# Attention and SwiGLU on one core: turning q and k of the last three sequences on VectorE instead of TensorE

## The chip, the cores and the metric

The kernel runs on one core of a Trainium2 chip. The metric is the device time of one execution in microseconds (us), as the median over several runs. The engines are named as the profile names them: PE is TensorE, with its weight loads (PEld) counted apart; DVE is VectorE, ACT is ScalarE, POOL is GpSimd, SP is SyncE, which here only issues DMAs (its queue is SPq). SBUF and PSUM have 128 partitions; matmuls write to PSUM, and DVE and ACT empty it.

## What is computed

Eight sequences of 448 rows with 12 heads of 64 columns. Queries and keys are normed row by row, attention follows, and the result of all heads, side by side, is the input of a SwiGLU layer:

```python
q_n = q / sqrt(mean(q*q) + 1e-6) * g_q        # k_n likewise, with g_k
attn = softmax(q_n @ k_n.T / sqrt(64))
x = (attn @ v), heads side by side            # 3584 rows of 768
xn = x / sqrt(mean(x*x) + 1e-6) * rms_g
out = (silu(xn @ w_gate) * (xn @ w_val)) @ w_out     # 768 -> 1536 -> 768
```

All data are float32.

## The kernel before, in words

**Groups and blocks.** Two heads make a group `g`, six groups a sequence `b` (`divmod(g, NPAIR)`), 48 groups in all. The main loop (line 1805) goes over the groups, one block of work each. From the second sequence on, a block begins with the attention of its group (`step`, line 677, seven parts: the scores of 64 keys against all 448 queries for both heads, the weighted sum of the group before, the exponentials), and the rest of the block is filled with pieces of the feed-forward layer of the sequence before (`fill`, line 1645). In block `g` the scores of group `g` are taken, the weighted sums of group `g - 1`, and groups `g + 1` to `g + 3` are made ready.

**Order by hand.** Every engine executes in the order in which the program issues. `pe(fn)` issues one piece of PE work and moves a clock `now["t"]` by one; `after(n, fn)` puts other work off by `n` such steps, so that it is issued behind later pieces. A block in the middle of a sequence has three calls of `fill`, about a third of its feed-forward work each.

**q and k before.** `load_pair` (line 407) loads rows 0 to 383 of q and k of a group, three rows to a partition; the last 64 rows of all heads of a sequence, the rests, are loaded once a sequence (`load_rests`, line 435). A q load has runs of 768 bytes (one DMA per group), a k load runs of 256 bytes (two DMAs). `squares` (line 484) squares on ACT, sums per row on DVE, and takes the power -1/2 on POOL (`rms_qk`, line 510); `norm_q` (line 517) scales q on POOL, `norm_k` (line 524) scales k on ACT, six instructions; `norm_rests` (line 450) does the same for the rests. `turn` (line 532) then turns rows into columns on PE: three transposes against the identity for q and one for the rests of both, and three for k, seven a group, into a PSUM bank, from which ACT copies them to `qT` (line 550, with the gains `gqk` as a column of scales) and `kT` (lines 551 and 553). The two turns of a group are two pieces of PE work in the block before its scores.

**Attention.** `scores` (line 655) multiplies 64 columns of kT by qT, two matmuls in the two halves of the array; `exps` (line 662) takes the exponential, without a maximum, since a bound on the scores was checked; `weighted` (line 666) multiplies by v. The sums of the exponentials are added up on POOL (`later_sums`, line 705) and over partitions on PE (`totals`, line 684).

**Feed-forward.** Gate and value products are made by a scheme with fewer multiplications (`product`, line 1180, line 1191 its matmuls, eight to a product), with additions on DVE and copies on ACT that empty the three PSUM banks for it (`ps_f`). The output layer has three forms; of these, the one in quadrants (`out_quads`, line 1476, matmuls in line 1532, `finish` with additions on POOL) runs under the attention of sequences 5 and 7 too. The weights, ready made, stream in from a scratch area in DRAM (`ask`, line 1042, DMAs in line 1070): a piece is asked for when a place in a ring of 22 pieces is free. All these DMAs are issued on SP, in one order with the loads of q, k and v and the stores of the output.

**v and the output.** v lies as q does, three rows to a partition, and the output rows (`store`, line 1347) follow that order.

## Time and profile before

| | |
|---|---|
| timed runs | 1516.35, 1512.67, 1513.35 us; median 1513.35 us |
| profiled execution, first to last instruction | 1514.0 us (no time around this span is given) |
| share of the span: PE, PEld, DVE, ACT, POOL | 98%, 76%, 69%, 40%, 49% |
| granted PE clock, mean | 0.997 |
| DMA share of 16 engines, by the SP queue | 69.4% |
| bytes moved, mean rate | 322.51 MB, 213 GB/s |

The profile is one execution. Busy times of an engine are the sums of its instructions' durations; matmuls overlap one another, so that a PE that is always busy is not yet a PE at its peak, and what a matmul costs is better read from the distance between starts in the timeline. A row of instruction groups reads: line, engine, operation, output and inputs with shapes, count, then the busy time in us and the mean ns of one, then the engine's idle time just before them and what ended it. A row of a stretch of time reads: from and to, length, busy us and count of PE, PEld, DVE, ACT and POOL, the granted clock, the DMA share, GB/s. A row of waits reads: who waited for whom, us in total, how often, the longest. A row of DMA issues reads: destination and source, queue, count, KB each, median us from issue to landing.

### The profile page before, as it was taken

What the parts mean: (1) busy time and instruction counts of PE and PEld (TensorE: products, weight loads), DVE (VectorE), ACT (ScalarE), POOL (GpSimd) and SP (SyncE); (2) the same over time, 40 slices, a digit from 0 to 9 for tenths busy, and PEclk for the clock granted to TensorE, in tenths of its full rate; (3) what the DMA queues carried; (4) which work ended last, traced back from release to release, by engine and by line L of the source; (5) the groups of instructions that cost most, each with busy time, mean ns of one, the idle gap of its engine ahead of it and who ended that gap; (6) DMA issues with size and microseconds to landing.
All of it is one profiled execution on the core that took longest, in us unless ns stands there. A gap on an engine that the chain in (4) does not pass through costs nothing.

```text
span 1514.0 us, 25709 instructions
## 1 busy us (share of the span) xinstructions
PE 1478.8 (98%) x8732; PEld 1154.0 (76%) x8732; DVE 1037.7 (69%) x1826; ACT 602.2 (40%) x1377; POOL 741.3 (49%) x708
## 2 busy tenths in 40 slices
PE   8999999999899999999999999999999999999997
PEld 4344445678755888878888888768888789899997
DVE  5788999699944697874568555535668655684664
ACT  6856764344323433234343443443542433101100
POOL 6867997556423454564535643445645731021002
PEclk9999999999999999999999999999999999999999
DMA  7758675776667899996558855585558655587675
GB/s 200 227 159 252 174 247 174 228 249 206 224 219 224 266 316 312 301 291 180 163 150 257 244 176 153 165 255 159 153 153 255 216 162 139 165 292 234 174 228 180
DMA packets 302176, 322.51 MB, mean 213 GB/s; under 512 B 81620, under 2 KB 243668, under 8 KB 302036
## 3 DMA queue, kind: packets, MB, share of 16 engines
q1 hardware_dynamic: 301108, 320.58, 69.4%
q8 instruction: 72, 1.18, 0.3%
q14 instruction: 68, 0.56, 0.1%
q10 hardware_dynamic: 800, 0.20, 0.1%
q0 software_dynamic: 128, 0.00, 0.0%
HBM read 266.90 MB, written 53.77 MB: 212 GB/s over the span
## 4 chain that ended last, share of the span: by engine, by line
PE 84%; DVE 8%; DMA 3%; issue 1%; SPq 1%; POOL 1%; ACT 0%; DVEq 0%; POOLq 0%
PE ff L1191 37%; PE ff L1532 13%; PE sc L659 7%; PE av L674 7%; PE ff L1604 6%; PE ff L1461 5%; PE tr L545 2%; PE den L692 1%; PE den L607 1%; PE sc L563 1%; PE av L590 1%; PE ff L1334 1%; DVE l L1406 1%; DMA w<-kept 1%; DVE w L1091 1%
## 5 line engine op out<-in xcount | busy, mean ns | idle before, releaser
L1191 PE MATMUL ff<-x,w 128*128 128x224 f32 x1296 | 259.6, 353 | 1.4 <-DVE pb L1212 1.1
L714 POOL TENSOR_TENSOR es<-es,e 128x448 f32<-128x448 f32 x205 | 253.4, 1236 | 13.6
L1191 PEld LDWEIGHTS ff<-x,w 128*128 128x128 f32 x1296 | 242.7, 190 | 5.4 <-DVE pb L1212 1.4
L659 PE MATMUL sc<-qT,kT 64*64 64x448 f32 x1176 | 231.0, 539 | 0.7 <-DVE x L744 0.7
L674 PE MATMUL av<-e,vt 64*64 64x448 f32 x984 | 193.1, 538 | 0.0
L664 ACT ACTIVATE e<-sc 128x448 f32<-128x448 f32 x294 | 154.2, 547 | 72.6 <-PE sc L659 57.1
L1191 PE MATMUL ff<-xs,w 128*128 128x224 f32 x832 | 165.0, 353 | 2.9 <-issue 1.6
L1191 PEld LDWEIGHTS ff<-xs,w 128*128 128x128 f32 x832 | 155.7, 190 | 6.2 <-issue 3.0
L644 POOL TENSOR_TENSOR ss<-ss,rd 128x448 f32<-128x448 f32 x40 | 47.1, 1178 | 207.2 <-ACT rd L643 206.5
L709 POOL TENSOR_TENSOR es<-e 128x448 f32<-128x448 f32 x41 | 49.2, 1200 | 192.3 <-ACT e L664 192.3
L659 PEld LDWEIGHTS sc<-qT,kT 64*64 64x64 f32 x1176 | 79.2, 133 | 82.1 <-issue 60.1
L1532 PE MATMUL ff<-w,l 128*128 128x192 f32 x630 | 117.8, 328 | 3.7 <-DVE pa L1567 1.7
L515 POOL TENSOR_TENSOR rs<-ms,mhalf 128x12 f32<-128x12 f32 (+1 forms) x50 | 115.9, 2319 | 4.2
L1212 DVE TENSOR_TENSOR pc<-ff,l 128x448 f32<-128x448 f32 x56 | 34.8, 622 | 115.7 <-PE ff L1191 80.9
L1604 PE MATMUL ff<-x,w 128*128 128x448 f32 x288 | 111.8, 541 | 0.0
L1532 PEld LDWEIGHTS ff<-w,l 128*128 128x128 f32 x630 | 103.8, 190 | 8.7 <-DVE pa L1567 2.9
L674 PEld LDWEIGHTS av<-e,vt 64*64 64x64 f32 x984 | 66.0, 133 | 41.6 <-issue 41.6
L1604 PEld LDWEIGHTS ff<-x,w 128*128 128x128 f32 x288 | 53.3, 190 | 51.1 <-issue 48.2
L1191 PE MATMUL ff<-top_x,w 128*128 128x224 f32 x440 | 91.1, 356 | 0.0
L1209 DVE TENSOR_TENSOR pb<-ff,pb 128x448 f32<-128x448 f32 x84 | 52.3, 623 | 56.1 <-PE ff L1191 50.3
L1191 PEld LDWEIGHTS ff<-top_x,w 128*128 128x128 f32 x440 | 81.8, 190 | 11.3 <-issue 8.5
L1191 PE MATMUL ff<-l,w 128*128 128x224 f32 x416 | 83.6, 353 | 1.1 <-DVE pc L1212 1.1
(212 smaller groups left out, 2806.1 us busy)
## 6 DMA issues: line engine op xcount, KB each, us to landing
w<-kept SPq DMA_DIRECT2D x380, 256.0 KB, 3.5
w<-kept_q SPq DMA_DIRECT2D x350, 192.0 KB, 3.8
w<-kept_o SPq DMA_DIRECT2D x150, 192.0 KB, 3.6
kept_q<-w SPq DMA_DIRECT2D x63, 192.0 KB, 3.9
qk<-in_q_dram SPq DMA_DIRECT2D x48, 192.0 KB, 3.7
qk<-in_k_dram SPq DMA_DIRECT2D x96, 96.0 KB, 3.7
raw<-in_moe_w_gate_dram SPq DMA_DIRECT2D x24, 384.0 KB, 4.8
raw<-in_moe_w_val_dram SPq DMA_DIRECT2D x24, 384.0 KB, 4.4
```

The source lines that it names most:

```text
L515: nc.gpsimd.tensor_tensor(st["rs", g][:, cols], ms, mhalf[:, cols], ALU.pow)
L644: after(m, lambda: (nc.gpsimd.tensor_tensor(ss, ss, rd, ALU.add), st.update({("summed", b): hp})))
L659: nc.tensor.matmul(ps[r, 0:S], lhsT=st["kT", g][r, keys_of(i)], rhs=st["qT", g][r, :], start=True, stop=True)
L664: nc.scalar.activation(e, ps[:, 0:S], ACT.Exp)
L674: nc.tensor.matmul(st["av", g][own(j), 0:S], lhsT=vt, rhs=st["e", g, i][r], start=i == 0, stop=i == PARTS - 1, skip_group_check=True)
L709: nc.gpsimd.tensor_tensor(st["es", g], st["e", g, 0], st["e", g, 1], ALU.add)
L714: nc.gpsimd.tensor_tensor(st["es", g], st["es", g], st["e", g, i], ALU.add)
L1191: nc.tensor.matmul(bank[:, w * HT:(w + 1) * HT], lhsT=data(key)[:, (2 * w + c) * 128:(2 * w + c + 1) * 128], rhs=a[left][:, c, :], start=o ...
L1209: nc.vector.tensor_tensor(T[name], ps[:, 0:S], T[name], ALU.add)
L1461: nc.tensor.matmul(ps, lhsT=left_o(b, which, LEFT_O[name], c), rhs=data(("wo", b, name, c)), start=first and c == 0, stop=c == NFP - 1, sk ...
L1532: nc.tensor.matmul(ps, lhsT=a[:, j, :], rhs=data(key)[:, n % 2 * HW:(n % 2 + 1) * HW], start=start and j == 0, stop=j == KG - 1, skip_grou ...
L1604: nc.tensor.matmul(bank[w][:, 0:S], lhsT=data(key)[:, c * 128:(c + 1) * 128], rhs=st["x", 0][:, 3 * half + c, :], start=half == c == 0, st ...
```

## The change

For the last three sequences (`b >= 5`, groups 30 to 47, `TURNED = 5`):

- A head's 448 rows are loaded 14 to a partition on 32 partitions, and by halves of 32 columns: partition block (head, half), 32 partitions each. q and k of a group become eight DMAs of 448 runs of 128 bytes, issued one per step of PE work, from four steps after the block's start.
- Each block of 32 partitions by 32 columns is then turned where it lies by one VectorE block transpose over 448 columns, one for q (in place) and one for k (into `kT`). q's columns come out in the order (row within partition, partition), and one ACT instruction reorders them, reading in steps of 32 words, and applies the gains. k's order is kept, and v is loaded in the same order of keys.
- The sum of squares is by halves. ACT exchanges the halves' sums between partitions (eight small copies), POOL adds them, takes the power over 21 columns and scales q over 448 columns. k isn't scaled: its factor goes into the exponential as a column of scales.
- No rests are loaded or normed for these sequences; v comes in four DMAs of 32 partitions; output rows are stored in the sequence's own order.
- q, k, v and the rests of all sequences now lie in one tile, `yard`, at places worked out by hand; for the first five sequences with as many buffers as before.
- The two turns are no longer pieces of PE work, so a block has two steps fewer. `squares` of group `g + 2` is issued behind the q turn of group `g + 1`, and v is loaded one block later (for group `g + 1` in block `g`).

The diff, cut to its core:

```diff
+    TURNED = 5
+    NB = S // 32
+    yard = slots.tile([128, AT_OTHER + PER_B], F32, name="yard")
...
+    def load_turned(g):
+        b, hp = divmod(g, NPAIR)
+        qk = st["qk", g] = spot(g % 3 * 2 * S, 2 * S).rearrange("p (a n) -> p a n", a=2)
+        def load(i, h, e):
+            to = (1 - h) * D + 32 * e
+            nc.sync.dma_start(out=blocks(qk[to:to + 32, i]),
+                              in_=(q, k)[i][b, 2 * hp + h].rearrange("(p c) d -> p c d", c=NB)[:, :, 32 * e:32 * e + 32])
+        for n in range(8):
+            after(4 + n, lambda n=n: load(n // 4, n // 2 % 2, n % 2))
...
+    def squares_turned(g):
...
+        for i in range(2):
+            sq = new_sq()
+            nc.scalar.activation(sq, qk[:, i], ACT.Square)
+            after(1, lambda i=i, sq=sq: nc.vector.tensor_reduce(out=ms[:, 0, i * NB:(i + 1) * NB], in_=blocks(sq), axis=AX_X, op=ALU.add))
...
+        def other():
+            for at in (0, 64):
+                nc.scalar.copy(ms[at:at + 32, 1, both], ms[at + 32:at + 64, 0, both])
+                for to, of in ((every, every), (first, second)):
+                    nc.scalar.copy(ms[at + 32:at + 64, 1, to], ms[at:at + 32, 0, of])
+                nc.scalar.copy(ms[at + 32:at + 64, 0, first], ms[at + 32:at + 64, 0, second])
+        def total():
+            nc.gpsimd.tensor_tensor(ms[:, 0, both], ms[:, 0, both], ms[:, 1, both], ALU.add)
+            nc.gpsimd.tensor_scalar(ms[:, 0, both], ms[:, 0, both], D * 1e-6, None, ALU.add)
+        def root():
+            nc.gpsimd.tensor_tensor(rs, ms[:, 0, both], mhalf, ALU.pow)
+            nc.gpsimd.tensor_tensor(blocks(qk[:, 0]), blocks(qk[:, 0]), rs[:, 0:NB].unsqueeze(2).to_broadcast([128, NB, 32]), ALU.mult)
+        after(2, other)
+        after(3, total)
+        after(3, root)
+    def turn_q(g):
...
+        q = st["qk", g][:, 0]
+        nc.vector.transpose(out=blocks(q), in_=blocks(q))
+        after(1, lambda: nc.scalar.activation(st["qT", g].rearrange("p (i n) -> p i n", n=NB), q.rearrange("p (n i) -> p i n", i=32),
+                                              ACT.Copy, scale=gqk[:, 0:1]))
+    def turn_k(g):
...
+        nc.vector.transpose(out=st["kT", g].rearrange("p (n s i) -> p s n i", s=2, i=32),
+                            in_=st["qk", g][:, 1].rearrange("p (s n i) -> p s n i", s=2, i=32))
...
     def exps(g, i, ps):
         e = st["e", g, i] = e_pool.tile([128, S], F32, name="e")
-        nc.scalar.activation(e, ps[:, 0:S], ACT.Exp)
+        if turned(g):
+            nc.scalar.activation(e, ps[:, 0:S], ACT.Exp, scale=st["rs", g][:, NB + i:NB + i + 1])
+        else:
+            nc.scalar.activation(e, ps[:, 0:S], ACT.Exp)
...
+    def turn_for(g, i):
+        if turned(g):
+            (turn_q, turn_k)[i](g)
+        else:
+            pe(lambda: turn(g, i))
...
         if hp:
             fill()
             norm_k(g + 1, 0)
-            squares(g + 2, 0)
-            squares(g + 2, 1)
-            pe(lambda: turn(g + 1, 0))
+            if not turned(g + 2):
+                squares(g + 2, 0)
+                squares(g + 2, 1)
+            turn_for(g + 1, 0)
+            if turned(g + 2):
+                squares(g + 2, 0)
             norm_k(g + 1, 1)
             some_rests(g)
             fill()
-            pe(lambda: turn(g + 1, 1))
+            turn_for(g + 1, 1)
             fill(hold=g % 2 == 1)
```

More of the change, by code (lines that the diff above doesn't have):

```diff
@@ new lines, in load_v_turned @@
+    def load_v_turned(g):
+        b, hp = divmod(g, NPAIR)
+        vt = st["v", g] = spot((AT_QK + 2 * PAIR, AT_V1)[g % 2], S).rearrange("p (n d) -> p n d", d=D)
+        for h in range(2):
+            rows = v[b, 2 * hp + h].rearrange("(p s n) d -> s p n d", s=2, n=NB // 2)
+            for half in range(2):
+                to = across(h).start + 32 * half
+                nc.sync.dma_start(out=vt[to:to + 32], in_=rows[half])
+    def squares_turned(g):
+        qk, n = st["qk", g], 2 * NB
+        ms = st["ms", g] = spot(AT_RS, 2 * n).rearrange("p (a n) -> p a n", a=2)
+        rs = st["rs", g] = spot(AT_RS + (4 + g % 2) * NB + g % 2 * NB // 2, NB + NB // 2)
+        for i in range(2):
+            sq = new_sq()
+            nc.scalar.activation(sq, qk[:, i], ACT.Square)
+            after(1, lambda i=i, sq=sq: nc.vector.tensor_reduce(out=ms[:, 0, i * NB:(i + 1) * NB], in_=blocks(sq), axis=AX_X, op=ALU.add))
+        every, first, second = slice(0, NB), slice(NB, NB + NB // 2), slice(NB + NB // 2, n)
+        both = slice(0, NB + NB // 2)
+        def other():
[13 more added lines that the diff above has]
+        after(3, root)
@@ L450, in norm_rests @@
     def norm_rests(b, lo, hi):
-        if b >= B:
+        if b >= TURNED:
             return
@@ L487, in squares @@
             return
+        if turned(g):
+            if i == 0:
+                squares_turned(g)
+            return
         n = 2 * NK
@@ L524, in norm_k @@
     def norm_k(g, half):
-        if g >= NG:
+        if g >= NG or turned(g):
             return
@@ L1878, in safe_scores @@
         st["block"] = now["t"]
-        after(2, lambda g=g: load_v(g + 2))
+        for n in (1, 2):
+            if turned(g + n) == (n == 1):
+                after(2, lambda g=g + n: load_v(g))
         if hp:
@@ L1894, in safe_scores @@
         fill(2)
-        pe(lambda: turn(g + 1, 0))
+        turn_for(g + 1, 0)
         norm_k(g + 1, 1)
@@ L1900, in safe_scores @@
         squares(g + 2, 1)
-        pe(lambda: turn(g + 1, 1))
+        turn_for(g + 1, 1)
         fill(len(todo))
```

70 lines of the change are left out of this document (52 added, 18 removed).

## The prediction

> **What bounds the kernel now.** I read the page's busy times first, then the table of busy time by stretches, then what TensorE (PE) waited for, then its timeline. The page says that PE is the fullest engine, which alone proves little, because its busy time is modelled:
>
> ```profile
> PE 1478.8 (98%) x8732; PEld 1154.0 (76%) x8732; DVE 1037.7 (69%) x1826; ACT 602.2 (40%) x1377; POOL 741.3 (49%) x708
> ```
>
> The change touches the groups (head pairs) 30 to 47. I asked for the stretch in which their transposes lie, whole, then for the two transposing lines in it, and for two shorter stretches:
>
> ```profile
> 745.00:1260.00 515.00, 512.77 (x3278) 431.12 (x3277) 318.21 (x548) 205.26 (x482) 254.60 (x239) 1.00 0.64 192
> 745.00:1260.00 515.00, 17.79 (x108) 14.05 (x108) 1.00 0.64 192
> 745.00:1260.00 515.00, 4.91 (x18) 2.54 (x18) 1.00 0.64 192
> 1020.00:1110.00 90.00, 90.00 (x569) 77.89 (x568) 53.31 (x85) 40.58 (x97) 48.43 (x49) 1.00 0.55 162
> 1110.00:1200.00 90.00, 89.33 (x613) 76.43 (x612) 71.65 (x129) 31.64 (x78) 51.96 (x45) 1.00 0.67 210
> ```
>
> The columns are PE, weight loads, DVE, ACT, POOL, granted clock, DMA share and GB/s. PE is idle for 515.0 - 512.77 = 2.2 us here, at full clock. The longest of its waits is this one:
>
> ```profile
> PE ff L1532 <- DVE pa L1567: 1.0, 2, 0.5
> ```
>
> So nothing but PE sets the pace of these 515 us, and PE work taken out of them shortens the kernel as long as no other engine or queue comes late. The second and third rows are the transposes of lines 545 and 549: 108 + 18 = 126 of them, seven for each of 18 groups, so the stretch holds exactly the transposes that go.
>
> **What is removed from PE.** Their busy time, 17.79 + 4.91 = 22.7 us, is not what they cost, since matmuls overlap. The timeline gives the cost as the distance between starts:
>
> ```profile
> 1043.31 1.68 PE L1191 MATMUL ff<-xs,w 128*128 128x224 f32 x8
> 1044.82 0.49 PE L545 MATMUL tr<-ident,qn 128*128 128x128 f32 x3
> 1045.15 0.27 PE L549 MATMUL tr<-ident,rest 128*128 128x128 f32 x1
> 1045.26 4.71 PE L1191 MATMUL ff<-xs,w 128*128 128x224 f32 x24
> ...
> 1051.32 0.49 PE L545 MATMUL tr<-ident,qk 128*128 128x128 f32 x3
> 1051.64 1.68 PE L1191 MATMUL ff<-top_x,w 128*128 128x224 f32 x8
> ```
>
> The q turn takes 1045.26 - 1044.82 = 0.44 us, the k turn 1051.64 - 1051.32 = 0.32 us, together 0.76 us a group and 18 x 0.76 = 13.7 us. Scores, weighted sums and denominators keep their matmuls, seven parts a group with the same shapes, so 13.7 us is all that PE can give. An eight-matmul product takes 1044.82 - 1043.31 = 1.51 us, which I need below as the measure of how late an engine that empties PSUM may be: there are three banks for the products.
>
> **What ScalarE (ACT) gets and loses.**
>
> ```profile
> L664 ACT ACTIVATE e<-sc 128x448 f32<-128x448 f32 x294 | 154.2, 547 | 72.6 <-PE sc L659 57.1 <-PE av L674 6.8 <-PE den L607 2.4
> L530 ACT ACTIVATE qk<-qk,rs 128x64 f32<-128x64 f32 x246 | 67.5, 344 | 0.0
> L912 ACT ACTIVATE raw<-raw 128x384 int32<-128x384 uint32 x72 | 40.7, 565 | 0.0
> L493 ACT ACTIVATE sq<-qk 128x384 f32<-128x384 f32 x96 | 45.0, 517 | 1.6 <-DMA qk<-in_k_dram 1.5
> L550 ACT ACTIVATE qT<-tr,gqk 128x448 f32<-128x448 f32 x48 | 30.3, 632 | 106.5 <-PE tr L549 106.5
> L567 ACT ACTIVATE e<-sc,rs 128x448 f32<-128x448 f32 x42 | 23.3, 638 | 13.3 <-PE sc L563 13.3
> L551 ACT COPY kT<-tr 128x64 f32<-128x64 f32 x40 | 8.1, 202 | 0.0
> ```
>
> Gone per group: six scalings of k (6 x 0.344), qT (0.632), the small copy of kT (0.202) and two squares (2 x 0.517), 3.9 us. I give no credit for the large copy of kT and the rests' work, which go too. New: two squares over 448 columns (0.517 x 448/384 = 0.60 each), eight small copies (at most 0.202 each, 1.6), seven exponentials that now take a scale from a column (0.638 against 0.547: 7 x 0.09 = 0.64), and the reordering of q. That last one reads in steps of 128 bytes, which no ACT row shows. Its lower end is L550's 0.632, the same size and the same column of scales; L912, which reads every second word, takes 565 ns against L493's 517, so a step costs little there. Its upper end comes from VectorE, the only engine here that reads in such steps:
>
> ```profile
> L597 DVE STREAM_TRANSPOSE rd<-rd 128x448 f32<-128x448 f32 x41 | 26.2, 639 | 55.1 <-ACT rd L699 54.8
> L598 DVE RECIPROCAL few<-rd 128x14 f32<-128x14 f32 x48 | 11.6, 243 | 1.6
> L496 DVE TENSOR_REDUCE ms<-sq 128x6 f32<-128x384 f32 x96 | 48.4, 543 | 29.3 <-ACT sq L493 29.3
> ```
>
> L598's 243 ns for 14 elements, were all of it the step, would make 448 x 17.4 ns = 7.8 us. I take 0.7 us, near L550, since 243 ns is about what any tiny instruction costs. ACT then has 1.2 + 1.6 + 0.64 + 0.7 = 4.1 us for the 3.9 and more that it loses, at 40.58 of 90 us busy: no change. The Trainium skill (SBUF — State Buffer, in "Door 1: The DMA port swizzle") speaks against this choice: SBUF works in 16-byte lines, and each access that crosses to a new line pays a penalty, of a size that it does not give. L912's step stays inside its lines, so no ACT row here tests the rule. By it the reordering lies nearer its upper end, and that is the slower rival below.
>
> The exponentials keep pace: by L664's row ACT sits idle 72.6/294 = 0.25 us before each, nearly always for PE's scores, and each grows by 0.09.
>
> **VectorE (DVE).** Two block transposes at L597's 0.639 = 1.28 us more per group; the two reductions grow by 448/384, 2 x 0.09 = 0.18 us. Together 1.5 us in a block of about 29 us (515 us / 18). Ahead of the transposes in DVE's order stand additions that empty PSUM; behind them stand others, and the next block's scores wait for kT and qT. In the gate and value stages DVE is busy 53.31 of 90 us, and k is turned about a third of a block, some 8 us of PE work, before its first use: that cover makes it free. In the output stage that works by quadrants (line 1532) DVE is at 71.65 of 90 and PE already waits for it (1.0 us above). Two such stages fall in this stretch; the chain of waits shows their first pieces, and the last matmul of the second one's weights comes from PE's timeline:
>
> ```profile
> 791.32 7.82 PE ff L1532 x48
> 1134.39 7.82 PE ff L1532 x48
> ```
>
> ```profile
> 1197.57 1.14 PE L1532 MATMUL ff<-w,l 128*128 128x192 f32 x6
> ```
>
> That is 64 us a stage, about four blocks in all. There the 1.5 us may cost nothing (they fit in DVE's gaps) or all of themselves, 4 x 1.5 = 6 us. I take 1.5 us in all, nearer to nothing, because the wait that exists is 1.0 us over the whole stretch.
>
> **GpSimd (POOL).**
>
> ```profile
> L714 POOL TENSOR_TENSOR es<-es,e 128x448 f32<-128x448 f32 x205 | 253.4, 1236 | 13.6
> L515 POOL TENSOR_TENSOR rs<-ms,mhalf 128x12 f32<-128x12 f32 x46 | 110.5, 2403 | 3.8
> ```
>
> The power goes from 12 to 21 columns, between 2.4 and 2.4 x 21/12 = 4.2 us; the scaling of q becomes one instruction over 448 columns, at most L714's 1.236, for two over 192; one tiny addition is new. That is under +3.0 us a group, even with nothing deducted for the two, on an engine at 254.60 of 515 us. It now waits for ACT's eight copies, which wait for DVE's reductions, and the additions of the output stage queue behind; but q is next touched a whole block later. Cost nothing.
>
> **The queue of DMA issues (SP).** Three q/k loads and two v loads become eight and four. Here is one block of the quadrant stage, where this queue is fullest, with the next block's first weights:
>
> ```profile
> 1146.97 1.31 SPq L432 DMA_DIRECT2D vt<-in_v_dram  x2
> 1148.33 8.59 SPq L1070 DMA_DIRECT2D w<-kept_q  x16
> 1158.19 2.12 SPq L1358 DMA_DIRECT2D out_dram<-y  x3
> 1160.40 9.42 SPq L1070 DMA_DIRECT2D w<-kept_q  x19
> 1170.09 0.38 SPq L414 DMA_DIRECT2D qk<-in_q_dram  x1
> 1170.57 1.27 SPq L418 DMA_DIRECT2D qk<-in_k_dram  x2
> 1171.94 1.50 SPq L1070 DMA_DIRECT2D w<-kept_q  x3
> 1177.55 1.32 SPq L432 DMA_DIRECT2D vt<-in_v_dram  x2
> 1178.92 4.15 SPq L1070 DMA_DIRECT2D w<-kept_q  x8
> ```
>
> From 1146.97 to the next v load at 1177.55 the queue issues for 24.6 of 30.6 us. New loads at 1.27/2 = 0.64 us each, v at 0.66: 8 x 0.64 + 4 x 0.66 - (0.38 + 1.27 + 1.31) = 4.8 us more, which still fits into the 6.0 us free. Weights are issued up to 1183 us and used up to 1198 us, so this queue runs about 14 us ahead, and being a few us late costs nothing. The moved bytes hardly matter:
>
> ```profile
> qk<-in_q_dram SPq DMA_DIRECT2D x48, 192.0 KB, 3.7
> qk<-in_k_dram SPq DMA_DIRECT2D x96, 96.0 KB, 3.7
> ```
>
> k's 256-byte runs land in the same 3.7 us as q's 768-byte runs, and a group's q and k are under 0.5 MB of the some 5 MB that a block moves. They are loaded two blocks ahead.
>
> **Sum.** 1514.0 - 13.7 + 1.5 = 1501.8 us on the profiled execution's span. The profile gives no time around that span; the three timed runs have their median 0.65 us below it, at 1513.35. Forecast: 1501.2 us.
>
> **Rivals.**
> *The issue queue becomes the bound.* If a load of 448 runs of 128 bytes on 32 partitions holds SP twice as long as a k load, 1.3 us, a quadrant block gets 8 x 1.3 + 2.6 - 3.0 = 10.0 us more for 6.0 free, and blocks are 0.8 us shorter: 4.8 us late per block, 9.6 us by the end of each of the two stages. The lead of 14 us at a stage's end, less 3.7 us of landing, would just cover that; if it is half as long inside the stage, 7 us, it covers 3.3, and PE gives back 2 x 6.3 = 12.6 us: 1513.8 us. For it: the queue is 80% full there. Against: issue time has grown slowly, 0.38 us for 256 runs and 0.64 for 384. The Trainium skill (DMA: Bandwidth & Descriptors, Specifications) asks for at least 512 bytes per transfer for line rate; by that the new loads are slow too, but k's 256-byte runs, already under it, show no later landing. 8%.
>
> *Slower: ACT's reordering holds PSUM.* ACT works in order, and the copies that empty the products' banks queue behind it. With three banks of 1.51 us, ACT may be late by two products, 3.0 us. Beyond that each us stops PE in each of 18 groups. It eats the 13.7 us at 3.8 us per reordering, and is slower by over 0.3% from 4.0 us on; at 5 us the time is 1501.2 + 18 x 2 = 1537 us. For it: the 7.8 us bound. Against: L912. 8%.
>
> *Nothing gained.* The transposes fill time in which PE would wait anyway, for instance for weights: 1513 us. The 2.2 us of idle time speak against it; for it, weights could arrive only just in time, which such a row doesn't show. 4%.
>
> *Every transpose costs its full busy time*, 22.7 us and not 13.7: 1492 us. The starts 0.11 us apart speak against it. 2%.
>
> **How the numbers follow.** The forecast has 78%; its own range is from 1499 (DVE costs nothing, and half a us of scatter) to 1506 (DVE costs all its 6 us). The range of 8 in 10 keeps both ends and takes in most of the first rival: 1498 to 1511. About 0.3%, 4.5 us, is what a measurement of this kernel can tell from no change, so faster means under 1508.8. Faster: forecast 78% and the last rival 2%, 80%. Same: 8% + 4% = 12%. Slower: 8%.
>
> **What would show it.** Right: no transposing matmul after about 750 us; PE's idle time in the stretch from there to the last scores still at 2 to 5 us; the stretch shorter by some 12 to 14 us. The reordering near 0.7 us, the block transposes near 0.64 us, q/k loads near 0.7 us each on SP. Wrong: PE waiting for ACT in the products (the second rival), for a landing of weights in the quadrant stages (the first), or for qT or kT at the front of a block, which I priced at nothing.

## The result, and the profile after

The changed kernel takes 1502.32 us (median of five runs, 1502.07 to 1507.69) against 1512.67 us for the kernel before in the same comparison (five runs, 1511.27 to 1516.35): a ratio of 0.9926, 95% interval 0.9911 to 0.9941. The forecast was 1501.2 us, with a range from 1498 to 1511. The profiled execution took 1502.07 us, 1.8 us more than its span of 1500.3 us.

The busy times of the page after, then of two stretches (columns as before). The first is the old one, cut to match the shorter kernel; the other is a piece of the quadrant stage:

```profile
PE 1466.1 (98%) x8606; PEld 1141.5 (76%) x8606; DVE 1056.0 (70%) x1856; ACT 609.7 (41%) x1371; POOL 758.6 (51%) x690
```

```profile
745.00:1248.00 503.00, 497.60 (x3139) 416.18 (x3138) 335.00 (x578) 209.97 (x467) 273.08 (x225) 1.00 0.68 196
1100.00:1190.00 90.00, 88.14 (x596) 75.06 (x595) 75.54 (x136) 33.53 (x78) 54.00 (x43) 1.00 0.74 218
```

PE executes 8732 - 8606 = 126 matmuls fewer, as said. But its idle time in the stretch rose from 2.2 to 503.00 - 497.60 = 5.4 us, and in the quadrant stage DVE went from 71.65 to 75.54 us busy of 90. These are PE's waits in that stretch:

```profile
PE ff L1653 <- DVE pb L1688: 1.2, 2, 0.6
PE ff L1653 <- DVE pa L1688: 1.1, 2, 0.6
PE ff L1653 <- DVE y L1673: 1.1, 2, 0.5
PE ff L1582 <- DVE y L1554: 0.6, 1, 0.6
PE ff L1582 <- ACT pa L1561: 0.6, 1, 0.6
PE ff L1653 <- DVE l L1527: 0.4, 2, 0.2
PE ff L1309 <- ACT pa L1324: 0.4, 1, 0.4
```

No landing of weights is among them. A product of the gate and value stage (line 1309) waits for ACT once, 0.4 us; another form of the output layer (line 1582) waits 0.6 us for ACT, as it did before. 3.8 of the 5.4 us are waits for DVE in the quadrant stage (line 1653, once line 1532), twice each: once per stage.

**Gain by block.** To place the gain I cut each trace at the first weighted sum of every block (numbered here by the group whose weighted sums it takes, one less than the loop's number). The cut points of blocks 28 and 46, first before, then after, are the first starts of these rows of the weighted sums:

```profile
L674 PE MATMUL av<-e,vt x8: 536/536/587, 738.8 to 739.9; 64*64 64x448 f32 x8
L674 PE MATMUL av<-e,vt x14: 536/536/587, 1263.6 to 1265.9; 64*64 64x448 f32 x14
```

```profile
L792 PE MATMUL av<-e,yard x8: 536/536/587, 736.5 to 737.7; 64*64 64x448 f32 x8
L792 PE MATMUL av<-e,yard x8: 536/536/587, 1251.7 to 1252.9; 64*64 64x448 f32 x8
```

So the 18 blocks in which the transposes lay went from 524.9 to 515.2 us. Of the 13.7 us by which the two profiles' spans differ, 9.7 are in this stretch, 2.2 ahead of it, and 1.8 behind it. Those ahead are scatter: the kernels below that differ little or nothing up to there reach the same point between 736.6 and 740.4 us. The gains against the kernel before, in us, of the changed kernel and of the twelve experiments (e1 to e12, in the order of the sections below; blocks 28, 29, 32 to 35, 37, 40, 41 and 45 gained 0.72 or 0.77 in all of them):

```
block    after   e1    e2    e3    e4    e5    e6    e7    e8    e9   e10   e11   e12
30       -0.52  0.33 -0.51 -0.52 -0.51 -0.46 -0.96 -0.52 -0.53 -0.62 -0.61 -0.52  0.33
31        0.59  0.31  0.63  0.61  0.65  0.05  0.32  0.59  0.60  0.33  0.33  0.60  0.65
36        0.44  0.44  0.44  0.44  0.44  0.44  0.19  0.44  0.44  0.17  0.18  0.44  0.44
38        0.77  0.57  0.77  0.77  0.77  0.77 -0.31  0.77  0.77  0.77  0.77  0.77  0.77
39        0.01  0.33  0.59  0.00  0.52  0.62 -1.48  0.01  0.01  0.11  0.11  0.01  0.53
42       -0.51  0.33 -0.50 -0.52 -0.51 -0.45 -0.95 -0.52 -0.53 -0.62 -0.61 -0.52  0.33
43        0.60  0.33  0.67  0.62  0.66  0.06  0.34  0.61  0.61  0.35  0.35  0.61  0.67
44        0.77  0.77  0.77  0.77  0.77  0.77  0.60  0.77  0.77  0.77  0.77  0.77  0.77
28-45     9.70 10.96 10.41  9.71 10.34  9.35  5.32  9.70  9.69  8.81  8.84  9.71 12.04
end       1.81 -0.19  1.96  1.85  2.04  1.93  1.84  1.06  1.62  1.71  1.64  2.00  1.76
```

Twelve of the 18 blocks give the 0.76 us of the forecast (0.72 or 0.77, 9.1 us together). Blocks 30, 31, 36, 39, 42 and 43 give 0.6 us together instead of 4.6. These 4.0 us are what the experiments had to explain; 30 and 31, 42 and 43 lie in the quadrant output stages of sequences 4 and 6, under the attention of 5 and 7. Timed comparisons have intervals of about 0.3%, some 4 us; in this stretch, blocks that a change doesn't touch agree to 0.02 us from trace to trace. So the verdicts below go by blocks. (Ahead of it they agree less well: block 22, untouched, is 0.2 to 1.6 us shorter than before in the kernels with `TURNED = 5`.)

### The profile page after: what moved, and what is told of

Read it like the earlier page. It is cut to its first block, busy times and chain, and to the rows that moved or that the text cites. A ratio compares the mean times of both kernels' runs of the same rounds, so it can differ in the third digit from the quotient of the medians.

```text
span 1500.3 us, 25709 instructions
## 1 busy us (share of the span) xinstructions
PE 1466.1 (98%) x8606; PEld 1141.5 (76%) x8606; DVE 1056.0 (70%) x1856; ACT 609.7 (41%) x1371; POOL 758.6 (51%) x690
## 4 chain that ended last, share of the span: by engine, by line
PE 82%; DVE 10%; DMA 3%; issue 2%; POOL 1%; ACT 1%; SPq 0%; DVEq 0%; POOLq 0%; ACTq 0%
PE ff L1309 37%; PE ff L1653 12%; PE sc L774 7%; PE av L792 7%; PE ff L1725 6%; PE ff L1582 5%; PE den L810 1%; DVE l L1527 1%; PE sc L674 1%; PE den L718 1%; PE av L701 1%; PE ff L1452 1%; PE tr L656 1%; DMA kept_o<-w 1%; DVE w L1209 1%
## 5 line engine op out<-in xcount | busy, mean ns | idle before, releaser
L792 PE MATMUL av<-e,yard 64*64 64x448 f32 x1148 | 223.9, 538 | 0.0
L792 PEld LDWEIGHTS av<-e,yard 64*64 64x64 f32 x1148 | 77.4, 133 | 50.0 <-issue 50.0
L782 ACT ACTIVATE e<-sc 128x448 f32<-128x448 f32 x168 | 87.8, 547 | 37.6 <-PE sc L774 28.0
L780 ACT ACTIVATE e<-sc,yard 128x448 f32<-128x448 f32 x126 | 76.6, 636 | 27.5 <-PE sc L774 21.5
L1624 POOL TENSOR_TENSOR y<-y,pa 128x384 f32<-128x384 f32 x10 | 11.4, 1157 | 149.1 <-DVE y L1700 124.6
```

The costliest lines, as they stand in the source:

```text
L780: nc.scalar.activation(e, ps[:, 0:S], ACT.Exp, scale=st["rs", g][:, NB + i:NB + i + 1])
L782: nc.scalar.activation(e, ps[:, 0:S], ACT.Exp)
L792: nc.tensor.matmul(st["av", g][own(j), 0:S], lhsT=vt, rhs=st["e", g, i][r], start=i == 0, stop=i == PARTS - 1, skip_group_check=True)
```

## The experiments

**e1: without PE's transposes alone.** The kernel before; the seven transposes of groups 30 to 47 are left out, and ACT's copies keep their sizes and read from SBUF instead, so qT and kT don't hold the turned data. It asks whether all of PE's transposes were on the path.

```diff
+        if g >= 30:
+            if i == 0:
+                nc.scalar.activation(st["qT", g].rearrange("p (n d) -> p n d", d=D), src[:, 0:D].unsqueeze(1).to_broadcast([128, S // D, D]),
+                                     ACT.Copy, scale=gqk[:, 0:1])
+                copy_k(st["kT", g][:, LAST], st["rest", b][:, hp].rearrange("p h d -> p (h d)")[:, D:])
+            else:
+                copy_k(st["kT", g][:, FULL], src)
+            return
```

> The kernel before, in which groups 30 to 47 have no transposes on PE: ACT copies the same number of columns from SBUF, unturned, so the output is not the reference's; DVE, POOL and the loads are as before. My theory: PE's 0.76 us a group can be had everywhere, and what the changed kernel misses of its 13.7 us is the price of the work that it adds to DVE and ACT. Then the fronts of blocks 29 to 47 come 13.7 us closer together, in the quadrant blocks too (0.77 us in each), and the time is near 1499. Rival: in the quadrant blocks DVE was the bound already, so that PE's time cannot be gained there whatever is added: then about 1.5 to 3 us of the 13.7 are missing here too, at the blocks in which the changed kernel gained nothing, and the time is near 1501 to 1502.

Measured: 1504.78 us, ratio 0.9932 [0.9915, 0.9950]; the stretch gives 10.96 us. So 2.7 us of the transposes were not on the path, within the 1.5 to 3 us of the rival: 0.44 in each of the blocks 30, 31, 39, 42 and 43, 0.33 in 36, 0.2 in 38. How a transpose can fill a wait is seen in PE's timeline of block 42, first before, then in e1 (line 1540 is line 1532 there):

```profile
1154.49 1.14 PE L1532 MATMUL ff<-w,l 128*128 128x192 f32 x6
1155.47 0.49 PE L545 MATMUL tr<-ident,qn 128*128 128x128 f32 x3
...
1155.90 1.16 PE L1532 MATMUL ff<-w,l 128*128 128x192 f32 x6
```

```profile
1147.35 1.14 PE L1540 MATMUL ff<-w,l 128*128 128x192 f32 x6
1148.67 1.24 PE L1540 MATMUL ff<-w,l 128*128 128x192 f32 x6 [0.19 <-DVE l L1414]
```

From `ff<-w,l` to `ff<-w,l` it is 1155.90 - 1154.49 = 1.41 us with the transposes and 1148.67 - 1147.35 = 1.32 without (the changed kernel has the same 1.32, and the same wait). Of the 0.44 us only 0.09 are won: the second product needs a sum `l` that DVE has only then. Before, nothing of this was to be seen as a wait, because the transposes stood in its place.

**e2: without DVE's block transposes.** The changed kernel; both are left out (kT is k as loaded).

```diff
-        nc.vector.transpose(out=blocks(q), in_=blocks(q))
...
-        nc.vector.transpose(out=st["kT", g].rearrange("p (n s i) -> p s n i", s=2, i=32),
-                            in_=st["qk", g][:, 1].rearrange("p (s n i) -> p s n i", s=2, i=32))
```

> The changed kernel without its two block transposes on DVE: q is reordered and k is read as they were loaded, so the output is not the reference's. All else stays. My theory: the transposes' 1.28 us a block cost time only where DVE is full, in the two stages by quadrants; the two blocks that gained nothing there (0.5 us longer than before each) gain 0.77 us each as the others do, the stretch becomes 2.5 to 3 us shorter, the time 1499.5. Rival 1 (DVE full without them): under 1 us gained. Rival 2 (ACT's reordering is what costs): under 0.5 us in the quadrant blocks, as the reordering is still there.

Measured: 1503.53 us, ratio 0.9929 [0.9910, 0.9948]; the stretch gives 10.41 us. Blocks 30 and 42 stay 0.5 us longer than before. The transposes cost 0.58 us in block 39, and nearly nothing elsewhere. The theory missed: what the quadrant blocks lose is something else.

**e3: q read straight.** The changed kernel; ACT copies q in the order in which it lies, so the scores get q's rows in a wrong order.

```diff
-        after(1, lambda: nc.scalar.activation(st["qT", g].rearrange("p (i n) -> p i n", n=NB), q.rearrange("p (n i) -> p i n", i=32),
-                                              ACT.Copy, scale=gqk[:, 0:1]))
+        after(1, lambda: nc.scalar.activation(st["qT", g], q, ACT.Copy, scale=gqk[:, 0:1]))
```

> The changed kernel with ACT reading q in a row instead of in steps of 128 bytes: the same instruction without the reordering, so the output is not the reference's. The changed kernel's reordering takes 1.09 us. My theory: the step costs 0.46 us of this, so that the instruction takes 0.63 here, and the only blocks in which it costs PE anything are the two outside the quadrant stages that gained less (0.77 and 0.33 us missing): about 1 us less, 1501.3. Rival: ACT's 0.46 us count in the quadrant blocks too, through the copy of a product's first quarter on ACT that DVE's additions wait for: then 2 to 3 us less.

Measured: 1504.38 us, ratio 0.9924 [0.9906, 0.9943]; 9.71 us. No block moves by more than 0.02 us, where 1 us or more had been expected. The instruction itself is shorter (ns, minimum, median and maximum, then the first and last start):

```profile
L495 ACT ACTIVATE qT<-yard,gqk x18: 667/668/673, 754.8 to 1241.6; 128x448 f32<-128x448 f32 x18
```

In the changed kernel its median is 1096 ns (below). So the stepped read costs time on ACT, and none of the kernel's.

**e4: both turns at the front of the block.**

```diff
+        if turned(g + 1):
+            turn_q(g + 1)
+            turn_k(g + 1)
```

(and not at their old places; the squares of group `g + 2` stay where they are.)

> The changed kernel with the turns of q and k of the next group issued at the block's front, right behind the attention steps, instead of after the first and the second third. Nothing is left out. DVE idles some 3 us there in the quadrant blocks (waiting for PE). My theory: the 1.28 us then lie in idle time and the quadrant blocks get most of their 0.77 us back, so 1.5 to 2.5 us less: 1500. Rival: DVE waits there for POOL's scaling of q, which ended between 4 us before and 3 us after the block's front in the changed kernel's trace, and holds up the additions that empty the banks: the same time or up to 5 us more.

Measured: 1502.25 us, ratio 0.9915 [0.9898, 0.9932]; 10.34 us. Block 39 gets 0.51 us back, 30 and 42 nothing, as in e2; that is less than half of the 1.5 to 2.5 us of the theory.

**e5: the row sums one step later.**

```diff
-            after(1, lambda i=i, sq=sq: nc.vector.tensor_reduce(out=ms[:, 0, i * NB:(i + 1) * NB], in_=blocks(sq), axis=AX_X, op=ALU.add))
+            after(2, lambda i=i, sq=sq: nc.vector.tensor_reduce(out=ms[:, 0, i * NB:(i + 1) * NB], in_=blocks(sq), axis=AX_X, op=ALU.add))
...
-        after(2, other)
-        after(3, total)
-        after(3, root)
+        after(3, other)
+        after(4, total)
+        after(4, root)
```

> The changed kernel with the row sums on DVE issued one step of PE work later (two instead of one behind the squares), ACT's exchange and POOL's power one step later too. Nothing is left out. Without the block transposes (the second experiment) the quadrant blocks still gained nothing, so the transposes are not what costs there. Theory now: the two reductions, 1.13 us, stand in DVE's order right ahead of the addition that empties the bank for which PE then waits 0.58 us; one step later they stand behind it, and blocks 30 and 42 (counted from nought by their fronts) gain 0.84 us more each, from -0.5 to +0.3 against before: 1.7 us. Rival: DVE is full there whatever the order, and the wait only moves: under 0.4 us in all.

Measured: 1503.76 us, ratio 0.9912 [0.9895, 0.9929]; 9.35 us. The wait in block 42 moves with the sums: matmul by matmul against the kernel before, the block is now ahead where it had lost 0.75 us, and loses 0.63 us some seven us later. Blocks 31 and 43 lose 0.54 more. The row sums are what is late there, but later is no better: as the rival said, the wait only moves.

**e6: the two steps kept.** The turns stay pieces of PE work without matmuls, and the squares stand where they stood before.

```diff
-            (turn_q, turn_k)[i](g)
+            pe(lambda: (turn_q, turn_k)[i](g))
...
-            if not turned(g + 2):
-                squares(g + 2, 0)
-                squares(g + 2, 1)
+            squares(g + 2, 0)
+            squares(g + 2, 1)
...
-            if turned(g + 2):
-                squares(g + 2, 0)
```

> The changed kernel in which the two turns keep their steps of the order by hand (empty for PE) and the squares stand ahead of the q turn again, so that all work put off by steps is issued where it was issued in the kernel before. Nothing is left out. Theory of order: blocks 30 and 42 gain the same 0.33 us as the kernel with no transposes on PE, not -0.5. Rival (DVE full whatever the order): they stay at -0.5, since the added 1.5 us of DVE work are all still there.

Measured, a single run: 1508.92 us; the stretch gives 5.32 us, 4.4 less than the changed kernel. Neither forecast held: blocks 30 and 42 do not gain 0.33 us, and lose 0.96 instead of 0.5. In block 42 DVE now has the turn of q (1152.93 us) and the row sums (1153.49 us) one behind the other, and PE loses 0.8 us at the matmul at which the changed kernel loses 0.75. DVE is late in more places, too:

```profile
PE ff L1653 <- DVE pa L1688: 3.2, 2, 1.6
...
PE ff L1309 <- DVE pc L1327: 1.2, 1, 1.2
```

This edit moves two things at once. That the steps and the squares' place together are worth 4.4 us here is shown; how it splits is not.

**e7: stores of at most 64 rows**, as the kernel before has them at its end.

```diff
-                m = min(S - col, row0 + 128 - at)
+                m = min(S - col, row0 + 128 - at, 64)
```

> The changed kernel with the output rows of the last three sequences stored in pieces of at most 64 rows. Nothing is left out. The changed kernel gains 1.8 us behind the last matmul, which the kernel with no transposes on PE does not. Theory: that is the last tiles' stores, three DMA issues there instead of four, since rows now lie in one piece; with pieces of 64 the 1.8 us go and nothing else changes. Rival: the 1.8 us come from where the last data lie in DRAM or SBUF; then they stay.

Measured, a single run: 1506.05 us, with a span of 1504.3 us; it reached block 28 at 739.8 us, 3.2 us later than the changed kernel, which is the scatter told of above. Its stretch is unchanged (9.70 us), and its end gives 1.06 us instead of 1.81. The last stores, before, after, and in e7, are:

```profile
1505.42 2.53 SPq L1358 DMA_DIRECT2D out_dram<-y  x4
```

```profile
1493.49 1.82 SPq L1479 DMA_DIRECT2D out_dram<-y  x3
```

```profile
1496.73 2.65 SPq L1479 DMA_DIRECT2D out_dram<-y  x4
```

One store fewer is worth 1.81 - 1.06 = 0.75 us at the end, less than half of what the theory put on it, where the kernels with an unchanged end have 1.62 to 2.04. The other 1.0 us lies in the closing sequence behind the last issue; its cause is open.

**e8: TURNED = 4**, so that sequence 4 is turned on DVE too; nothing else differs from the changed kernel.

> The changed kernel with four sequences turned on DVE instead of three. Nothing is left out. The six groups more have their turns in blocks under the output stage by quadrants of sequence 2, so by the accounts of the three sequences: about 6 x 0.77 less 1.3 to 1.8, 2.8 to 3.3 us more gained, 1499. Rival: DVE is busier in that stretch (67 of 80 us between 600 and 680 us) and issues ahead of the weights there were only 3.9 us early; then nothing or less than nothing is gained.

Measured: 1515.63 us, ratio 0.9998 [0.9985, 1.0011]. The stretch gives 9.69 us as ever; what is lost lies ahead of it, where sequence 4 is loaded and turned. Blocks 21 to 25 are 1.2, 3.6, 2.0, 4.9 and 0.4 us longer than in the changed kernel. PE's waits between 430 and 760 us show the landings of weights that the first rival of the prediction named (in the changed kernel they are 1.0 us there):

```profile
PE ff L1653 <- DMA w<-kept_q: 4.8, 7, 1.3
PE ff L1309 <- DMA w<-kept: 2.9, 2, 2.7
```

There the weights for the quadrant form are still being made on DVE and stored by SP (`derive_q`), beside the stream of weights; waits for DVE come on top, 6.4 us there against 2.8 in the changed kernel.

**e9: all at the front.** e4, and the squares of group `g + 2` at the block's front too; the row sums are issued at the first third without waiting for a step.

```diff
+        if turned(g + 2) and g + 2 < NG:
+            for i in range(2):
+                sq = st["sq", g + 2, i] = new_sq()
+                nc.scalar.activation(sq, st["qk", g + 2][:, i], ACT.Square)
...
-            sq = new_sq()
-            nc.scalar.activation(sq, qk[:, i], ACT.Square)
-            after(1, lambda i=i, sq=sq: nc.vector.tensor_reduce(out=ms[:, 0, i * NB:(i + 1) * NB], in_=blocks(sq), axis=AX_X, op=ALU.add))
+            nc.vector.tensor_reduce(out=ms[:, 0, i * NB:(i + 1) * NB], in_=blocks(st.pop(("sq", g, i))), axis=AX_X, op=ALU.add)
```

> Both turns, and also the squares of group g + 2, are issued at the block's front; VectorE's row sums then follow at the first third without waiting for a step. Nothing is left out of the computation. Theory (in the quadrant blocks 30 and 42 VectorE has one gap of about 1 us, into which the row sums' 1.1 us fit if nothing else is put there and if they are there in time): blocks 30 and 42 go from 0.5 us longer than before to 0.3 us shorter, 31 and 43 stay within 0.1 us, the stretch from block 29 to block 47 is about 1.7 us shorter than with the turns alone at the front (514.54 us), the time about 1500.5 us. Rival (VectorE is simply full in these blocks, wherever the work stands): 30 and 42 stay 0.5 us longer, the stretch 514.5 us, the time 1502 us.

(Its "stretch from block 29 to block 47" counts by the loop's numbers; it is the one of the table.)

Measured: 1505.60 us, ratio 0.9942 [0.9929, 0.9956]; 8.81 us, the worst of the re-orderings, and blocks 30 and 42 lose 0.62. By these numbers alone the theory had fallen. But the loss sits elsewhere: at the place where the changed kernel loses 0.75 us in block 42, nothing is lost now, and 0.87 us are lost some six us earlier. GpSimd and DVE, from the end of block 41 on, show where it began:

```profile
1127.36 0.94 POOL L480 TENSOR_TENSOR yard<-yard 128x448 f32<-128x448 f32 x1
1136.72 1.14 POOL L826 TENSOR_TENSOR es<-e 128x448 f32<-128x448 f32 x1 [8.43 <-ACT e L779]
1137.94 4.15 POOL L831 TENSOR_TENSOR es<-es,e 128x448 f32<-128x448 f32 x3
```

```profile
1127.43 1.34 DVE L1340 SCALAR_TENSOR_TENSOR h<-th,pb 128x448 f32<-128x448 f32 x1
...
1136.89 1.39 DVE L1526 TENSOR_TENSOR l<-l,top 128x384 f32<-128x384 f32 x1
1138.20 1.49 DVE L1526 TENSOR_TENSOR h<-top,h 128x384 f32<-128x384 f32 x1
1139.62 1.48 DVE L1498 TENSOR_TENSOR raw<-raw,top 128x384 f32<-128x384 f32 x1
```

In e4 the same four DVE instructions take 0.61, 0.55, 0.55 and 0.55 us. With the row sums earlier, GpSimd scales q earlier (at 1129.00 us in e4, which stands 0.44 us ahead of e9 there) and starts 0.07 us ahead of DVE's line 1340, which takes 1.34 us for 0.61. That makes DVE 0.7 us late; 9 us on, the first of its three additions starts behind GpSimd's first `es` instead of ahead of it, and the two engines then take turns: DVE's additions start 1.31 and 1.42 us apart, GpSimd's three take 4.15/3 = 1.38 us each. That is 1.39 + 1.49 + 1.48 - 3 x 0.55 = 2.7 us more on DVE, of which PE feels the 0.87.

**e10: the row sums in the step of their squares.** e4, with the two reductions issued directly behind the two squares.

```diff
+        sqs = [new_sq() for i in range(2)]
...
-            after(1, lambda i=i, sq=sq: nc.vector.tensor_reduce(out=ms[:, 0, i * NB:(i + 1) * NB], in_=blocks(sq), axis=AX_X, op=ALU.add))
+            nc.scalar.activation(sqs[i], qk[:, i], ACT.Square)
+        for i in range(2):
+            nc.vector.tensor_reduce(out=ms[:, 0, i * NB:(i + 1) * NB], in_=blocks(sqs[i]), axis=AX_X, op=ALU.add)
```

> Both turns at the block's front; the row sums are issued directly behind their squares, in the same step. Nothing is left out of the computation. Theory (the row sums are late by one step): blocks 30 and 42 about 0.3 us shorter than before instead of 0.5 us longer, the stretch about 513 us. Rival (VectorE then stands waiting for ScalarE's squares of 0.6 us each, in every block): the blocks in which VectorE empties PSUM just in time lose up to 0.6 us each, the stretch 515 us or more.

Measured: 1504.61 us, ratio 0.9931 [0.9917, 0.9945]; 8.84 us, block by block the same as e9 to 0.01 us, so that the theory missed here too. GpSimd's work comes early here as well, for the same reason. The rival's price was nearly the one measured, but not for its reason: DVE didn't stand waiting for ACT's squares in blocks 30 and 42.

**e11: TURNED = 4 with the steps kept** for groups 24 to 29.

```diff
-    TURNED = 5
+    TURNED = 4
...
+            if g < 5 * NPAIR:
+                pe(lambda: (turn_q, turn_k)[i](g))
+            else:
+                (turn_q, turn_k)[i](g)
```

> TURNED = 4, but for groups 24 to 29 the two turns keep their steps of PE work, so that the order of the feed-forward pieces and the making of the quadrant weights go on as in the kernel before. Nothing is left out of the computation. Theory A (two steps fewer a block push the making of these weights together): blocks 21 to 24, which were 1.2 to 4.9 us longer than in the changed kernel with TURNED = 4, come back to within 1 us, the time about 1503 us. Theory B (the queue of DMA issues is full there, and the eight loads of a group hold up the weights): they stay 2 us and more longer each, TensorE waits for landings of weights, the time about 1514 us.

Measured, a single run: 1511.61 us. Block 24 comes back (1.4 us longer than in the changed kernel instead of 4.9), and 22 gets worse (5.8 instead of 3.6; the granted clock between 560 and 748 us was 0.98 in this execution, against 1.00 between 560 and 740 us in the changed kernel's). The waits for landings are down to 0.5 us, and another has come:

```profile
PE ff L1309 <- DVE w L1275: 5.5, 1, 5.5
```

```profile
560.00:748.00 188.00, 177.00 (x1107) 152.29 (x1110) 139.64 (x251) 69.73 (x159) 93.95 (x78) 0.98 0.85 248
```

Neither theory held: the landings of e8 did go when the steps were kept, so that the queue is not bound to be too full, but then PE waits 5.5 us for a sum of weights (`w`, line 1275) on DVE. A part of the loss is the clock: it was granted at 0.50 from 582.7 to 586.1 and from 613.4 to 616.8 us here, and from 586.7 to 590.1 us in e8, each time at the end of a wait of PE of 2.7 to 5.5 us; the changed kernel has no such piece in these blocks. At half the rate, 3.4 us are 1.7 us of work lost, each time. Why TURNED = 4 brings nothing stays open beyond this: it meets the making of the quadrant weights, on DVE and on SP.

**e12: the row sums early for two groups.** e4, with the row sums in the step of their squares for groups 33 and 45 alone, whose squares fall into blocks 30 and 42.

```diff
+            sums = lambda i=i, sq=sq: nc.vector.tensor_reduce(out=ms[:, 0, i * NB:(i + 1) * NB], in_=blocks(sq), axis=AX_X, op=ALU.add)
+            if g % 12 == 9:
+                sums()
+            else:
+                after(1, sums)
```

> Both turns at the block's front, as in the fourth kernel; the row sums are issued in the same step as their squares for the groups 33 and 45 alone (those whose squares fall into blocks 30 and 42), one step later for all others. Nothing is left out of the computation. Theory (VectorE's additions that touch SBUF alone and GpSimd's instructions take turns, and blocks 30 and 42 lose only because the row sums come one step late into a crowded place; with all row sums early, GpSimd's scaling of q in block 41 came early too, met an addition of VectorE, made it 0.7 us late, and then three more additions took turns with GpSimd's and lost 2.8 us): GpSimd's work in block 41 is where it was, so blocks 30 and 42 go from 0.5 us longer than before to 0.3 us shorter, all others stay as with the turns at the front, the stretch is 512.9 us. Rival (these blocks have no room for VectorE's added work wherever it stands): they stay at 0.5 us longer or lose elsewhere in the block, the stretch is 514.5 us or more.

Measured: 1500.78 us, ratio 0.9916 [0.9901, 0.9931]; 12.04 us, a stretch of 512.84 us where 512.9 were expected. Blocks 30 and 42 gain 0.33, all others are as in e4. DVE's order in block 42 shows the step, before, after, and in e12:

```profile
1156.68 0.62 DVE L772 TENSOR_TENSOR xs<-x 128x448 f32<-128x448 f32 x1
1157.21 1.01 DVE L496 TENSOR_REDUCE ms<-sq 128x6 f32<-128x384 f32 x2
1158.14 0.35 DVE L1557 TENSOR_TENSOR th<-ff,th 128x192 f32<-128x192 f32 x1
...
1160.86 0.55 DVE L1567 TENSOR_TENSOR pb<-ff,th 128x384 f32<-128x384 f32 x1
```

```profile
1146.38 0.61 DVE L890 TENSOR_TENSOR xs<-x 128x448 f32<-128x448 f32 x1
1146.91 0.64 DVE L494 STREAM_TRANSPOSE yard<-yard 128x448 f32<-128x448 f32 x1
1147.77 0.36 DVE L1678 TENSOR_TENSOR th<-ff,th 128x192 f32<-128x192 f32 x1 [0.22 <-PE ff L1653]
...
1150.56 1.13 DVE L464 TENSOR_REDUCE yard<-sq 128x14 f32<-128x448 f32 x2
1151.62 0.54 DVE L1688 TENSOR_TENSOR pb<-ff,th 128x384 f32<-128x384 f32 x1
```

```profile
1145.00 0.61 DVE L894 TENSOR_TENSOR xs<-x 128x448 f32<-128x448 f32 x1
1145.53 1.14 DVE L464 TENSOR_REDUCE yard<-sq 128x14 f32<-128x448 f32 x2
1146.58 0.35 DVE L1682 TENSOR_TENSOR th<-ff,th 128x192 f32<-128x192 f32 x1
...
1149.17 0.54 DVE L1692 TENSOR_TENSOR pb<-ff,th 128x384 f32<-128x384 f32 x1
```

Ahead of the instruction `th<-ff,th` (lines 1557, 1678, 1682) DVE would wait for PE (0.78 us in e4, where the place is empty). Before, the row sums stood there; in the changed kernel the q turn has the place, with 0.22 us to spare, and the sums, one step later, stand ahead of the addition into `pb`, which empties PSUM, and make it 1.1 us late. PE waits for it (0.6 us, in the first row of its waits). With the sums back in the place, PE's wait is gone. Against e4 the trace is 1.7 us shorter, against the changed kernel 2.3 us (515.18 to 512.84). The timed intervals of the three overlap, so the gain over the changed kernel rests on the traces; over the kernel before it is clear.

## Why the prediction was right, and where it was not

The forecast was that PE's time goes and little comes back: 12.2 us shorter on the span. The stretch and the end together give 9.7 + 1.8 = 11.5 us in the traces, the medians 1512.67 - 1502.32 = 10.4. (The time is not under the span, as the prediction had it: every run on record takes 1.7 to 2.0 us more than its span, so the profile before showed an execution of about 1515.8 us, slower than the median. The difference that was forecast doesn't rest on this.) Of the signs that it named, the stretch "shorter by some 12 to 14 us" did not come, it is 9.7; PE's idle time there, 5.4 us, is just outside 2 to 5; and one product waits for ACT, 0.4 us. By its steps:

- **PE gives 13.7 us: too much by 1.7.** Twelve blocks give 0.72 or 0.77 us, as said. But the rival "nothing gained: the transposes fill time in which PE would wait anyway", priced at all or nothing, holds in part of them. e1 shows 2.7 us of it in the order of the kernel before; in e12, the best order found, 13.7 - 12.0 = 1.7 us are still missing, half of it the 0.33 instead of 0.77 in blocks 30 and 42; there, and in block 36 (0.44), e12 gains just what e1 gains, in which no engine has the added work. The step that failed is the conclusion from PE's 2.2 us of idle time that nothing else sets the pace: an engine that comes in time only because PE does something else first leaves no row of waits.
- **DVE's 1.5 us: 2.3.** This is the difference between the changed kernel and e12, which has the same work on DVE in another order. The place was right for most of it (1.7 us in the quadrant blocks 30 and 42) and the size within the bounds of 0 to 6, but it was not the transposes that came late there (e2, e4): it was the row sums, issued one step of PE work later because the turn of q was no longer a step. In the gate and value stage the transposes were called free, by the time until kT is used; in block 39 they cost 0.5 us (e2, e4), by another way. DVE's row sums stand behind the turn of q, ACT's eight small copies wait for these sums (0.53 us in e3), and behind them stands ACT's copy `pa` out of a bank, for which PE waits 0.36 us.
- **ACT's reordering, 0.7 us: 1.10.** These are rows of instructions after:

```profile
L495 ACT ACTIVATE qT<-yard,gqk x18: 1071/1096/1107, 751.0 to 1237.9; 128x448 f32<-128x448 f32 x18
L494 DVE STREAM_TRANSPOSE yard<-yard x18: 630/635/637, 750.4 to 1237.2; 128x448 f32<-128x448 f32 x18
L480 POOL TENSOR_TENSOR yard<-yard,mhalf x18: 3721/3722/4075, 726.6 to 1211.6; 128x21 f32<-128x21 f32 x18
```

  Against e3's 668 ns for the same 448 elements of the same tile in a row, the step of 128 bytes costs 1.10 - 0.67 = 0.43 us, 1 ns an element, against the 17 ns of the upper bound. This pair of rows tests what the Trainium skill (SBUF — State Buffer, Door 1: The DMA port swizzle) says of a penalty for crossing 16-byte lines: it agrees, and the size that the page leaves open is small. That it costs the kernel nothing is shown by e3, and the slower rival falls with it. The block transposes take 0.635 us where 0.639 were put, the power 3.7 us within 2.4 to 4.2; GpSimd's work is hidden as said, except through DVE (next section).
- **The queue of DMA issues: nothing, right.** A q/k load holds SP for 0.57 us, where 0.64 were put, v's four for 2.69. The lines are SP's, then the landings:

```profile
1137.40 2.69 SPq L454 DMA_DIRECT2D yard<-in_v_dram  x4
...
1141.08 0.57 SPq L440 DMA_DIRECT2D yard<-in_q_dram  x1
```

```profile
yard<-in_q_dram SPq DMA_DIRECT2D x72, 56.0 KB, 3.0
yard<-in_k_dram SPq DMA_DIRECT2D x72, 56.0 KB, 3.5
```

  With TURNED = 5 no weights are waited for in the stretch; with 4 they are, where sequence 4 is turned (e8), so the rival was about a real danger, one sequence away.
- **The end was not priced:** 1.8 us, of which 0.75 is one store fewer (e7).
- **The two steps fewer were not priced:** the whole order of DVE's work moved with them, and e6, which keeps them with the squares' old place, gives 4.4 us back. The row sums' step, on which e5, e10 and e12 turn, is a part of the same thing.

So the sum came out near by luck in part: PE's gain, 1.7 us too high, and DVE's price, 0.8 us too low, met a gain that was left out (the end's 1.8). It is chance, too, that the spans of the two profiles differ by the very 13.7 us of PE's term: 2.2 us of that are scatter ahead of the stretch.

## What to carry to other kernels

Work that is taken from a full engine pays only where no other engine is just in time behind it: ask of each piece what its successor waits for besides the piece, which a table of the waits before can't show. Where an engine has one gap in a stage, the question for added work is not how long it is but who had the gap before: here 1.1 us of sums pushed one step on cost 0.84 us a block, and giving them the gap back and the transposes another place removed it. Judge such edits of tenths of a us by blocks in the trace, since the timed runs scatter by more than all of them together.

## What was unexpected in the hardware

DVE's additions of two SBUF operands and GpSimd's instructions go one after the other. In the changed kernel, 163 of DVE's 244 additions over 384 columns in lines 1499 and 1527 meet no instruction of GpSimd in time; their median is 0.550 us and the longest takes 0.559. The 57 that lie for over nine tenths of their time beside GpSimd's have a median of 0.955 and reach 1.489 us. The row of one group of these, and of an addition that reads PSUM and one SBUF operand:

```profile
L1527 DVE TENSOR_TENSOR l<-h,h x20: 546/553/1482, 592.6 to 1469.2; 128x384 f32<-128x384 f32 x20
L1678 DVE TENSOR_TENSOR th<-ff,th x35: 317/356/360, 612.9 to 1488.5; 128x192 f32<-128x192 f32 x35
```

The addition that reads PSUM never stretches (at most 0.360 us), nor does the block transpose above (0.637), though 23 of the 35 and 8 of the 18 lie beside GpSimd's instructions in the same way. The Trainium skill (SBUF — State Buffer, SBUF: two separate sides) states it so: DVE and GpSimd share a pair of ports under an exclusive lock, which a DVE instruction with two SBUF inputs needs against a GpSimd instruction that reads SBUF, and whichever starts first has it for its whole instruction while the other blocks. The rows agree, and e9 shows what it does to a schedule: 0.07 us between two starts decided who waited, and cost DVE 0.7 us at once and 2.7 us more some nine us later, so that moving work by one step on one engine moved the loss to a place that the edit had not touched.
